# The second product of 43 token tiles by seven half-size products (Strassen), with the block sums of the squares on VectorE

## Chip, cores, metric

One core of one Trainium2 chip. The metric is the device time of one launch in microseconds (us); lower is better. Engines: TensorE (PE; PEld is its weight load), VectorE (DVE), ScalarE (ACT), GpSimd (POOL), and SyncE (SP), which here only issues DMAs.

## What is computed

The input is 8 sequences of 3008 positions with 256 channels. Each is Fourier transformed along its positions, mixed over the channels with complex weights, soft-thresholded and transformed back. The 8 x 3008 = 24064 results are tokens of a dense layer with a squared-ReLU:

```python
X = np.fft.rfft(x, axis=1)
Yr = Xr @ w_r - Xi @ w_i + b_r           # and Yi alike
Yr = np.sign(Yr) * np.maximum(np.abs(Yr) - 0.01, 0.0)
y = np.fft.irfft(Y, n=3008, axis=1).reshape(24064, 256)
r = np.maximum(y @ w_in, 0.0)            # w_in 256 x 2048: the first product
out = (s * (r * r) + b) @ w_out          # w_out 2048 x 256: the second product
```

The second product holds for g = r * r alone: s and the constant b times the column sums of w_out are brought in when the result leaves PSUM (s_bc, bias_bc).

## The kernel before

**Transforms.** 3008 = 94 x 32, so a transform is two stages of small matrix products with a transposition through DRAM between them. The work on batch b comes in units: s1_units (first forward stage, tile u, line 582), s23_units (second forward stage L618, channel mixing L633 and L647, soft threshold on VectorE L652 to L659 in the tile ring, first inverse stage L677) and s4_units (last inverse stage L730, tile yt). Most results leave PSUM through evac (L170 on ScalarE, L174 on VectorE). The first batch is transformed ahead of everything by first_batch, in the first 46 us. Units take their PSUM banks from one_bank (psf, two banks).

**Dense layer.** The tokens are cut into 48 tiles, mostly 512 tokens: 12 "wide" tiles (batches 0 and 1, of 512 or 480 tokens), 30 "main" tiles and 6 "tail" tiles (of 512 or 384), in the order of _tile_order. For tile ti, first_mm(ti, mc) computes one of MC = 16 blocks of 128 hidden features: two matmuls of 512 columns (L781) into half of a two-bank PSUM tile psh (two of those). After every second block ScalarE takes the ReLU of both into rt (f32, three buffers, L788), and the square goes to gt (f16), on VectorE (L795) or on ScalarE (L792). A tile's gt is eight buffers of 1024 columns; there are 15.

The second product of tile ti-1 runs while tile ti's first product does. Its stationary operand is gt, 128 features by up to 128 tokens, its moving operand a 256-column row block of w_out (L852). A sub-tile of 128 (or 120) tokens takes 16 matmuls that accumulate in half of a bank psa (two banks); two sub-tiles share a bank. VectorE then forms psa * s + bias into ost (L862), and SP stores it.

**Order.** The loop at the end writes the order by hand. Each tile has 16 slots, one for each mc: a slot issues the planned units of the transforms, then first_mm, then its share of the other tile's second product, four matmuls:

```python
for mc in range(MC):
    if ti < ti_n:
        for u in plan.pop(ti * MC + mc, []):
            u()
        first_mm(ti, mc)
    for u in nxt[mc * per_slot : (mc + 1) * per_slot]:
        u()
```

Where a job could go to either of ScalarE and VectorE, a planner decides when the program is built: load holds the time booked on both, and the job goes where its end is earlier by the planner's costs. For the squares:

```python
if load["act"] + 0.25 + w / 600.0 < load["dve"]:
    nc.scalar.activation(out=gt[:, :, 0:w], in_=rt[:, :, 0:w], func=AF.Square)
```

Each engine runs its instructions in order. When the program is built, the instructions of one engine may still change places with neighbours that they don't depend on.

Of the kernel before, what the change touches and what calls it, by code (L numbers as in the profile page):

```python
# [9 lines left out]
F16 = mybir.dt.float16  # L10
F32 = mybir.dt.float32
# [85 lines left out]
def kernel(  # L97
# [99 lines left out]
    def other_bank():  # L197
        return apool.tile([P, 512], F32, name="psa", tag="psa")
# [5 lines left out]
    def emit_load_x(b, first=None):  # L204
        xv = x[b].rearrange("(n1 n2) d -> n1 (n2 d)", n2=N2)
        for c in range(N2 // XCH):
            t = xpool.tile([P, XCH * D], F16, name="x16", tag="x16")
# [29 lines left out]
        nc.sync.dma_start(out=st, in_=w.rearrange("(c p) e -> p c e", p=P))  # L237
        w_st.append(st)

    b_g = cpool.tile([P, 2, D], F32, name="b_g")  # L240
# [6 lines left out]
    b_h = cpool.tile([P, D], F16, name="b_h")  # L247
# [4 lines left out]
    sel_t = cpool.tile([P, P], F16, name="sel_t")  # L252
    eye_t = cpool.tile([P, P], F16, name="eye_t")
    C_t = cpool.tile([96, 96], F16, name="C_t")

    b_st = rpool.tile([P, 2, D], F32, name="b_st", tag="rt")
# [79 lines left out]
            nc.vector.tensor_copy(out=blocks(F_2[0])[r, q, 1, a], in_=F_c[r, q, 0])  # L336


    w_sum = cpool.tile([P, 2, D], F16, name="w_sum")

    def sum_w_out():
        acc = opool.tile([P, 2, D], F32, name="acc", tag="ost")
# [6 lines left out]
    def make_bias():  # L349
        ps = other_bank()  # L350
        for i in range(2):
            nc.tensor.matmul(ps[:, 0:D], ones, w_sum[:, i], start=(i == 0), stop=(i == 1))
        nc.scalar.activation(out=bias_bc, in_=ps[:, 0:D], func=AF.Copy, scale=bb_bc)

    us = {}
    vs = {}
# [358 lines left out]
    def s4_units(b):  # L715

        groups = []
        for lo in range(0, N2, 5):
            for ec in range(DC):
                groups.append((lo, min(5, N2 - lo), ec))  # L720

        def unit(g):
            n2, w, ec = groups[g]
            if g == 0:
                yts[b] = ypool.tile([P, DC, N2, 96], F16, name="yt", tag="yt")
            yt = yts[b]
            ps = one_bank()
            for j in range(w):
                h, k = divmod(n2 + j, HW)
                nc.tensor.matmul(  # L730
                    ps[:, j * 96 : (j + 1) * 96],
                    vs[(b, h)][:, k, ec * P : (ec + 1) * P], C_t,
                    start=True, stop=True,
                )
            evac(
                yt[:, ec, n2 : n2 + w, :],
                ps[:, 0 : w * 96].rearrange("p (j n) -> p j n", n=96), w * 96,
            )
# [29 lines left out]
    def first_mm(ti, mc):  # L768
        tl = tiles[ti]
        w = width(tl)  # L770
        if mc % 2 == 0:
            hold_h["ps"] = two_banks()
        ps = hold_h["ps"]
        for dc in range(DC):
            o = ps[:, mc % 2, 0:w]
            r = rhs_of(tl, dc)
            if tl[0] == "main":
                o = o.rearrange("p (n m) -> p n m", m=16)
            if tl[0] == "wide":
# [8 lines left out]
        nc.scalar.activation(out=rt[:, :, 0:w], in_=ps[:, :, 0:w], func=AF.Relu)  # L788
        gt = gpool.tile([P, 2, 512], F16, name="gt", tag="gt")
        load["act"] += 0.17 + w / 600.0  # L790
        if load["act"] + 0.25 + w / 600.0 < load["dve"]:
            nc.scalar.activation(out=gt[:, :, 0:w], in_=rt[:, :, 0:w], func=AF.Square)  # L792
            load["act"] += 0.25 + w / 600.0
        else:
            nc.vector.tensor_tensor(  # L795
                out=gt[:, :, 0:w], in0=rt[:, :, 0:w], in1=rt[:, :, 0:w], op=ALU.mult
            )
            load["dve"] += 0.15 + w / 480.0
        gts[(ti, mc // 2)] = gt

    def store(tl, sub, src):
        kind, b, j, w = tl
        if kind == "wide":
# [33 lines left out]
    def second_mms(ti):  # L837

        tl = tiles[ti]
        w = width(tl)  # L840
        size = sub_size(tl)
        nsub = -(-w // size)
        hold = {}

        def mm(sub, mc):

            alone = ti == len(tiles) - 1 and sub >= 2
            h = 0 if alone else sub % 2
            if h == 0 and mc == 0:
                hold["ps"] = other_bank().rearrange("p (h e) -> p h e", h=2)  # L850
            ps = hold["ps"]
            nc.tensor.matmul(  # L852
                ps[0:size, h, :], gts[(ti, mc // 2)][:, mc % 2, sub * size : (sub + 1) * size],
                w_out_t[:, mc, :],
                start=(mc == 0), stop=(mc == MC - 1),
            )
            if sub == nsub - 1 and mc % 2 == 1:
                gts.pop((ti, mc // 2))
            if mc == MC - 1 and (alone or h == 1 or sub == nsub - 1):
                k = h + 1  # L860
                ost = opool.tile([P, 2, D], F32, name="ost", tag="ost")
                nc.vector.scalar_tensor_tensor(  # L862
                    out=ost[0:size, 0:k], in0=ps[0:size, 0:k], scalar=s_bc[0:size],
                    in1=bias_bc[0:size].unsqueeze(1).to_broadcast([size, k, D]), op0=ALU.mult, op1=ALU.add,
                )
# [4 lines left out]
        return [lambda s=s, m=m: mm(s, m) for s in range(nsub) for m in range(MC)]  # L870
# [24 lines left out]
    schedule(17, 10, rest[4:])  # L895
    plan.setdefault(14, []).append(make_bias)
    plan.setdefault(18, []).append(load_x_2)
    schedule(24, 42, s23_units(1))
    schedule(mark[1] - 12, 16, s4_units(1))
    for b in range(2, B):  # L900
# [8 lines left out]

    ti_n = len(tiles)  # L910
    for ti in range(ti_n + 1):
        nxt = second_mms(ti - 1) if ti else []
        per_slot = -(-len(nxt) // MC)
        for mc in range(MC):
            if ti < ti_n:
                for u in plan.pop(ti * MC + mc, []):
                    u()
                first_mm(ti, mc)
            for u in nxt[mc * per_slot : (mc + 1) * per_slot]:
                u()  # L920
    assert not plan

# [29 lines left out]
```

## Time and profile before

| | |
|---|---|
| three timed runs | 846.21, 847.24 (median), 849.21 us |
| span of the profiled execution | 844.6 us; the median run is 2.6 us longer, what lies around the span |
| PE busy | 835.1 us (99%), clock granted 1.00 but for the first 46 us (0.96) |
| VectorE, ScalarE busy | 694.7 us (82%), 640.6 us (76%) |
| main loop, 46 to 831 us | 785.2 us: PE 784.0, VectorE 654.5, ScalarE 604.0 |
| matmuls of the second product (L852) | 3024 |
| squares on VectorE, on ScalarE | 319, 65 |
| HBM traffic | 119 GB/s over the span |

Busy time is the union of an engine's instructions, so where two overlap they count once. A duration is from start to end; on TensorE, VectorE and ScalarE the next independent instruction starts before that end, and the distance between starts is what an instruction costs its engine.

### The profile page before, as it was taken

Reading aid. Unit: us, or ns where it says so; the run is one execution under the profiler, and the core shown is the slowest. Engines: PE = TensorE matmul, PEld = TensorE weight load, DVE = VectorE, ACT = ScalarE, POOL = GpSimd, SP = SyncE. Lnnn points to the kernel's source line nnn. Section 1 sums busy time; section 2 is a strip of 40 time slices with the busy share of each in tenths; the row PEclk is TensorE's granted clock in tenths of the full one; section 3 lists DMA queues with packets and bytes.
Section 4 is the critical chain, followed back from the end, with each engine's and each line's share of the span. In section 5 each row is a group of like instructions: output and inputs, shape, how many; then the busy total and the mean of one; then the engine's idle time right before and its main releaser. Section 6 shows DMA issues by size and latency. Waiting matters only on the chain.

```text
span 844.6 us, 17119 instructions
## 1 busy us (share of the span) xinstructions
PE 835.1 (99%) x6654; PEld 601.3 (71%) x6654; DVE 694.7 (82%) x1034; ACT 640.6 (76%) x862; POOL 45.9 (5%) x73
## 2 busy tenths in 40 slices
PE   8999999999999999999999999999999999999998
PEld 7857767777677766777677776777667777766765
DVE  5999987888888988888888888798978888776674
ACT  5987887778778877788777787778877778666673
POOL 4630000000000001000000000000000000000000
PEclk9999999999999999999999999999999999999999
DMA  7955467224851367324761247613354223411111
GB/s 200 181 151 118 119 161 199 74 77 98 202 156 54 103 171 188 93 70 107 189 174 50 81 101 196 172 43 90 106 152 125 59 78 97 113 33 38 38 44 50
DMA packets 105939, 96.06 MB, mean 114 GB/s; under 512 B 9607, under 2 KB 97675, under 8 KB 104515
## 3 DMA queue, kind: packets, MB, share of 16 engines
q1 hardware_dynamic: 99362, 80.55, 32.9%
q0 software_dynamic: 6496, 14.42, 10.6%
q8 instruction: 52, 0.85, 0.4%
q14 instruction: 29, 0.23, 0.1%
HBM read 53.52 MB, written 46.66 MB: 119 GB/s over the span
## 4 chain that ended last, share of the span: by engine, by line
PE 92%; ACT 3%; DVE 2%; DMA 1%; issue 1%; POOL 0%; DVEq 0%; ACTq 0%; POOLq 0%
PE psa L852 38%; PE psh L781 37%; PE psf L647 4%; PE psf L582 3%; PE psf L633 2%; PE psf L677 2%; PE psf L618 2%; PE psf L730 2%; ACT rt L788 1%; DMA x<-in_x_dram 1%; PE psm L425 1%; POOL x L213 0%; ACT yt L170 0%; DVE z L463 0%; PE psf L456 0%
## 5 line engine op out<-in xcount | busy, mean ns | idle before, releaser
L788 ACT ACTIVATE rt<-psh 128x1024 f32<-128x1024 f32 (+2 forms) x384 | 387.2, 1009 | 120.2 <-PE psh L781 118.8
L795 DVE TENSOR_TENSOR gt<-rt 128x1024 f16<-128x1024 f32 (+2 forms) x319 | 382.3, 1202 | 94.4 <-ACT rt L788 93.4
L852 PE MATMUL psa<-w_out_t,gt 128*128 128x256 f16 (+1 forms) x3024 | 454.4, 272 | 0.1
L852 PEld LDWEIGHTS <-gt 128*128 128x128 f16 (+1 forms) x3024 | 300.9, 101 | 186.6 <-issue 1.1
L781 PE MATMUL psh<-yt,w_in 128*128 128x512 f16 (+1 forms) x1344 | 396.8, 378 | 0.2 <-ACT rt L788 0.2
L781 PEld LDWEIGHTS <-w_in 128*128 128x128 f16 x1536 | 142.7, 98 | 26.2 <-issue 1.2
L862 DVE SCALAR_TENSOR_TENSOR ost<-psa,s_bc,bias_bc 128x512 f32<-128x512 f32 (+2 forms) x97 | 71.1, 733 | 9.6 <-PE psa L852 7.9
L792 ACT ACTIVATE gt<-rt 128x1024 f16<-128x1024 f32 (+2 forms) x65 | 68.2, 1050 | 0.9
L652 DVE TENSOR_TENSOR ring<-psf,s 128x512 f16<-128x512 f32 x84 | 57.6, 685 | 3.3 <-PE psf L647 3.2
L170 ACT CAST v<-psf 128x512 f16<-128x512 f32 x77 | 44.8, 582 | 19.4 <-PE psf L677 19.4
L170 ACT CAST xf<-psf 128x512 f16<-128x512 f32 x79 | 46.3, 586 | 8.8 <-PE psf L618 8.8
L781 PE MATMUL psh<-tail,w_in 128*128 128x512 f16 (+1 forms) x192 | 52.1, 353 | 0.0
L170 ACT CAST u<-psf 96x512 f16<-96x512 f32 x74 | 42.8, 580 | 11.2 <-PE psf L582 10.9
L647 PE MATMUL psf<-W_g,xf 128*128 128x256 f16 x336 | 50.4, 273 | 0.0
L170 ACT CAST yt<-psf 128x480 f16<-128x480 f32 (+2 forms) x76 | 39.0, 520 | 14.7 <-PE psf L730 14.2
L213 POOL DMA_DIRECT2D x<-in_x_dram x36 | 18.8, 527 | 432.9 <-PE psf L582 431.7
L582 PE MATMUL psf<-x,A_t 94*96 94x512 f16 x102 | 38.9, 382 | 1.0 <-ACT yt L170 0.6
L658 DVE TENSOR_TENSOR ring<-ring,high 128x512 f16<-128x512 f16 x84 | 35.6, 423 | 2.3
L659 DVE TENSOR_TENSOR ring<-ring 128x512 f16<-128x512 f16 x84 | 35.6, 423 | 2.1
L657 DVE TENSOR_TENSOR ring<-ring,low 128x512 f16<-128x512 f16 x84 | 35.5, 422 | 1.6
L647 PEld LDWEIGHTS <-xf 128*128 128x128 f16 x336 | 32.9, 98 | 4.1 <-issue 0.2
L730 PE MATMUL psf<-C_t,vs 96*128 96x96 f16 x448 | 33.2, 205 | 0.0
(100 smaller groups left out, 508.6 us busy)
## 6 DMA issues: line engine op xcount, KB each, us to landing
out_dram<-ost SPq DMA_DIRECT2D x152, 128.0 KB
ud<-u SPq DMA_DIRECT2D x28, 384.0 KB
us<-ud SPq DMA_DIRECT2D x28, 384.0 KB
vd<-v SPq DMA_DIRECT2D x42, 256.0 KB
vs<-vd SPq DMA_DIRECT2D x14, 768.0 KB
x<-in_x_dram POOLq DMA_DIRECT2D x28, 376.0 KB, 6.3
ring<-ring SPq DMA_DIRECT2D x280, 32.0 KB
out_dram<-ost SPq DMA_DIRECT2D x16, 120.0 KB
```

The costliest lines, as they stand in the source:

```text
L170: return None, nc.scalar.copy(out=dst, in_=src)
L582: nc.tensor.matmul(ps[0:96, :], A_t[0:N1, :], x16[(b, c)][0:N1, j * D : (j + 2) * D], start=True, stop=True,)
L647: nc.tensor.matmul(ps[:, r, :], xt[:, 2 - r, dc], W_g[:, dc, r], start=(dc == 0), stop=(dc == DC - 1),)
L652: nc.vector.tensor_tensor(out=t, in0=ps, in1=hold[i // 2][:, i % 2].unsqueeze(1).to_broadcast([P, 2, D]), op=ALU.add,)
L658: nc.vector.tensor_tensor(out=m, in0=m, in1=high, op=ALU.min)
L730: nc.tensor.matmul(ps[:, j * 96 : (j + 1) * 96], vs[(b, h)][:, k, ec * P : (ec + 1) * P], C_t, start=True, stop=True,)
L781: nc.tensor.matmul(o, w_in_t[dc][:, mc * P : (mc + 1) * P], r, start=(dc == 0), stop=(dc == DC - 1),)
L788: nc.scalar.activation(out=rt[:, :, 0:w], in_=ps[:, :, 0:w], func=AF.Relu)
L792: nc.scalar.activation(out=gt[:, :, 0:w], in_=rt[:, :, 0:w], func=AF.Square)
L795: nc.vector.tensor_tensor(out=gt[:, :, 0:w], in0=rt[:, :, 0:w], in1=rt[:, :, 0:w], op=ALU.mult)
L852: nc.tensor.matmul(ps[0:size, h, :], gts[(ti, mc // 2)][:, mc % 2, sub * size : (sub + 1) * size], w_out_t[:, mc, :], start=(mc == 0), sto ...
L862: nc.vector.scalar_tensor_tensor(out=ost[0:size, 0:k], in0=ps[0:size, 0:k], scalar=s_bc[0:size], in1=bias_bc[0:size].unsqueeze(1).to_broad ...
```

## The change

For 43 tiles (all of 512 or 480 tokens but the first and the last tile) the second product is seen as a 2 x 2 block product. The tile's tokens are halved (i), its 16 feature blocks are split into even and odd ones (k: the two that share a square), and the 256 output columns are halved. With A(i,k) the squares and B(k,j) the weights, Strassen's method in Winograd's form needs seven products of half size in every direction instead of eight:

- s_op makes four block sums of the squares in f16 on VectorE, each in two halves q of the features: S1 = A21 + A22 into new buffers s1, S3 = A11 - A21, S2 = S1 - A11 and S4 = A12 - S2 in place of blocks of gt.
- make_t makes the four block differences T of w_out once, on GpSimd.
- seven_mms issues 7 products x 2 sub-tiles x 8 feature blocks = 112 matmuls of 128 columns, seven per slot, into four bank fills per tile (psa still has two banks); leave(bank) then adds up the products with seven scaled adds from PSUM (add) and two adds in SBUF (both) per tile.
- The first tile, the last one, and the tail tiles of 384 tokens keep second_mms.
- gt becomes buffers of half a tile (four). To make room, the pools of x, u, xf and v lose one buffer each, and some constants share buffers. yt is computed with 94 columns per position rather than 96.

The planner books the new VectorE work, 0.07 + size / 480 for a block sum, 0.4 for add, 0.35 for both. The core of the diff:

```diff
-    xpool = ctx.enter_context(tc.tile_pool(name="xp", bufs=4))
-    upool = ctx.enter_context(tc.tile_pool(name="up", bufs=3))
+    xpool = ctx.enter_context(tc.tile_pool(name="xp", bufs=3))
+    x2pool = ctx.enter_context(tc.tile_pool(name="xp2", bufs=1))
+    upool = ctx.enter_context(tc.tile_pool(name="up", bufs=2))
-    xfpool = ctx.enter_context(tc.tile_pool(name="xfp", bufs=4))
+    xfpool = ctx.enter_context(tc.tile_pool(name="xfp", bufs=3))
-    vpool = ctx.enter_context(tc.tile_pool(name="vp", bufs=3))
+    vpool = ctx.enter_context(tc.tile_pool(name="vp", bufs=2))
-    gpool = ctx.enter_context(tc.tile_pool(name="gp", bufs=15))
-    opool = ctx.enter_context(tc.tile_pool(name="op", bufs=3))
+    gpool = ctx.enter_context(tc.tile_pool(name="gp", bufs=4))
+    opool = ctx.enter_context(tc.tile_pool(name="op", bufs=4))
+    spool = ctx.enter_context(tc.tile_pool(name="sp", bufs=2))
+    zpool = ctx.enter_context(tc.tile_pool(name="zp", bufs=1))
...
+    def w_block(k, j):
+        return w_out_t.rearrange("p (q k) d -> p q k d", k=2)[:, :, k, j * P : (j + 1) * P]
+
+    def make_t(i):
+        if not T_s:
+            T_s.append(x2pool.tile([P, 4, MC // 2, P], F16, name="T_s", tag="x2"))
+        t = T_s[0]
+        a, b = (
+            (w_block(0, 1), w_block(0, 0)),
+            (w_block(1, 1), t[:, 0]),
+            (w_block(1, 1), w_block(0, 1)),
+            (w_block(1, 0), t[:, 1]),
+        )[i]
+        nc.gpsimd.tensor_tensor(out=t[:, i], in0=a, in1=b, op=ALU.subtract)
...
-        gt = gpool.tile([P, 2, 512], F16, name="gt", tag="gt")
+        q, g = divmod(mc // 2, 4)
+        if g == 0:
+            gts[(ti, q)] = gpool.tile([P, 4, 2, 512], F16, name="gt", tag="gt")
+        gt = gts[(ti, q)][:, g]
...
+    def part(ti, q, i, k):
+        size = 2 * sub_size(tiles[ti])
+        return gts[(ti, q)][:, :, k, i * size : (i + 1) * size]
+
+    def s_op(ti, n, q):
+        size = 2 * sub_size(tiles[ti])
+        if n == 1:
+            sums[(ti, q)] = spool.tile([P, 4, 2 * P], F16, name="s1", tag="s1")
+        s1 = sums[(ti, q)][:, :, 0:size]
+        a11, a12, a21, a22 = (part(ti, q, i, k) for i in range(2) for k in range(2))
+        out, a, b, op = {
+            1: (s1, a21, a22, ALU.add),
+            3: (a21, a11, a21, ALU.subtract),
+            2: (a11, s1, a11, ALU.subtract),
+            4: (a12, a12, a11, ALU.subtract),
+        }[n]
+        nc.vector.tensor_tensor(out=out, in0=a, in1=b, op=op)
+        load["dve"] += 0.07 + size / 480.0
+
+    def seven_mms(ti):
+        left = [("g", 0, 0), ("g", 0, 1), ("s", 0, 0), ("g", 0, 0), ("g", 1, 0), ("g", 1, 1), ("g", 0, 1)]
+        right = [w_block(0, 0), w_block(1, 0)] + [T_s[0][:, i] for i in (0, 1, 2, 3)] + [w_block(1, 1)]
+
+        def mm(n, j, c):
+            if n % 2 == 0 and j == 0 and c == 0:
+                hold[n // 2] = other_bank().rearrange("p (n j e) -> p n j e", n=2, j=2)
...
+            nc.tensor.matmul(
+                hold[n // 2][0:size, n % 2, j], lhs, right[n][:, c],
+                start=(n % 2 == 0 and j == 0 and c == 0), stop=(c == MC // 2 - 1),
+                skip_group_check=True,
+            )
+
+        def add(out, n, other):
+            nc.vector.scalar_tensor_tensor(
+                out=out, in0=hold[n // 2][0:size, n % 2], scalar=s_bc[0:size],
+                in1=other, op0=ALU.mult, op1=ALU.add,
+            )
+            load["dve"] += 0.4
+
+        def both(out, a, b):
+            nc.vector.tensor_tensor(out=out, in0=a, in1=b, op=ALU.add)
+            load["dve"] += 0.35
...
+            if bank == 0:
+                add(c22, 0, wide(bias_bc))
+                add(c11, 1, c22)
+            elif bank == 1:
+                add(c22, 3, c22)
+                add(z, 2, wide(b_21))
+                both(c12, c22, z)
+            elif bank == 2:
+                add(c22, 4, c22)
+                add(c21, 5, c22)
+                both(c22, c22, z)
+                for j in range(2):
+                    store(tl, 2 + j, hold["o", 1][:, j, :])
+            else:
+                add(c12, 6, c12)
+                for j in range(2):
+                    store(tl, j, hold["o", 0][:, j, :])
+
+        C = MC // 2
+        order = [(n, j, c) for n in range(2) for j in range(2) for c in range(C - 1)]
+        order += [(n, j, C - 1) for n in range(2) for j in range(2)]
+        order += [(n, j, c) for n in range(2, 7) for j in range(2) for c in range(C)]
+        slots = [[] for _ in range(MC)]
+        for at, what in enumerate(order):
+            slots[at // 7].append(lambda w=what: mm(*w))
+        for at, n, q in ((3, 1, 1), (4, 3, 1), (4, 2, 0), (5, 2, 1), (7, 4, 0), (8, 4, 1)):
+            slots[at].append(lambda n=n, q=q: s_op(ti, n, q))
+        for at, bank in ((6, 0), (9, 1), (13, 2), (15, 3)):
+            slots[at].append(lambda bank=bank: leave(bank))
+        return slots
...
+        if ti:
+            nxt = seven_mms(ti - 1) if seven(ti - 1) else second_mms(ti - 1)
...
                 first_mm(ti, mc)
+                if mc in (9, 10) and seven(ti):
+                    s_op(ti, 1 if mc == 9 else 3, 0)
```

In the changed kernel's line numbers, s_op's instruction is L922, the 128-column matmul L944, add L951, both L958, the square on VectorE L826, the first product L809.

More of the change, by code (lines that the diff above doesn't have):

```diff
@@ L206, in emit_load_x @@
         for c in range(N2 // XCH):
-            t = xpool.tile([P, XCH * D], F16, name="x16", tag="x16")
+            if b < 2 and c == N2 // XCH - 1:
+                t = x2pool.tile([P, XCH * D], F16, name="x2", tag="x2")
+            else:
+                t = xpool.tile([P, XCH * D], F16, name="x16", tag="x16")
             if first is not None:
@@ L238 @@
         w_st.append(st)
-    b_g = cpool.tile([P, 2, D], F32, name="b_g")
+    b_g = tpool.tile([P, 2, D], F32, name="b_g", tag="tail")
+    small = tpool.tile([P, 4, D], F16, name="small", tag="tail")
     nc.vector.memset(b_g, 0.0)
@@ L246 @@
     F_2 = [uspool.tile([P, H, P], F16, name="F_2", tag="us") for _ in range(2)]
-    b_h = cpool.tile([P, D], F16, name="b_h")
+    b_h = small[:, 0]
     nc.vector.memset(b_h, 0.0)
@@ L251 @@
         nc.gpsimd.dma_start(out=b_h[64 * i : 64 * i + 1], in_=bv.unsqueeze(0))
-    sel_t = cpool.tile([P, P], F16, name="sel_t")
-    eye_t = cpool.tile([P, P], F16, name="eye_t")
+    sel_t = small[:, 1, 0:P]
+    eye_t = small[:, 1, P:D]
     C_t = cpool.tile([96, 96], F16, name="C_t")
@@ L336, in place_f @@
             nc.vector.tensor_copy(out=blocks(F_2[0])[r, q, 1, a], in_=F_c[r, q, 0])
-    w_sum = cpool.tile([P, 2, D], F16, name="w_sum")
+    w_sum = small[:, 2:4]
+    b_21 = cpool.tile([P, P], F32, name="b_21")
+    T_s = []
+    def w_block(k, j):
[11 more added lines that the diff above has]
+        nc.gpsimd.tensor_tensor(out=t[:, i], in0=a, in1=b, op=ALU.subtract)
     def sum_w_out():
@@ L353, in make_bias @@
         nc.scalar.activation(out=bias_bc, in_=ps[:, 0:D], func=AF.Copy, scale=bb_bc)
+        nc.gpsimd.tensor_tensor(
+            out=b_21, in0=bias_bc[:, P:D], in1=bias_bc[:, 0:P], op=ALU.subtract
+        )
     us = {}
@@ L730, in unit @@
                 nc.tensor.matmul(
-                    ps[:, j * 96 : (j + 1) * 96],
-                    vs[(b, h)][:, k, ec * P : (ec + 1) * P], C_t,
+                    ps[:, j * N1 : (j + 1) * N1],
+                    vs[(b, h)][:, k, ec * P : (ec + 1) * P], C_t[:, 0:N1],
                     start=True, stop=True,
@@ L735, in unit @@
             evac(
-                yt[:, ec, n2 : n2 + w, :],
-                ps[:, 0 : w * 96].rearrange("p (j n) -> p j n", n=96), w * 96,
+                yt[:, ec, n2 : n2 + w, 0:N1],
+                ps[:, 0 : w * N1].rearrange("p (j n) -> p j n", n=N1), w * N1,
             )
@@ L798, in first_mm @@
             load["dve"] += 0.15 + w / 480.0
-        gts[(ti, mc // 2)] = gt
     def store(tl, sub, src):
@@ L839, in second_mms @@
         tl = tiles[ti]
-        w = width(tl)
         size = sub_size(tl)
-        nsub = -(-w // size)
+        nsub = -(-tl[3] * (16 if tl[0] == "wide" else 1) // size)
         hold = {}
@@ L852, in mm @@
             nc.tensor.matmul(
-                ps[0:size, h, :], gts[(ti, mc // 2)][:, mc % 2, sub * size : (sub + 1) * size],
+                ps[0:size, h, :],
+                gts[(ti, mc // 8)][:, mc // 2 % 4, mc % 2, sub * size : (sub + 1) * size],
                 w_out_t[:, mc, :],
@@ L856, in mm @@
             )
-            if sub == nsub - 1 and mc % 2 == 1:
-                gts.pop((ti, mc // 2))
             if mc == MC - 1 and (alone or h == 1 or sub == nsub - 1):
@@ L868, in mm @@
                     store(tl, sub - k + 1 + i, ost[:, i, :])
-        return [lambda s=s, m=m: mm(s, m) for s in range(nsub) for m in range(MC)]
+        units = [lambda s=s, m=m: mm(s, m) for s in range(nsub) for m in range(MC)]
+        per_slot = -(-len(units) // MC)
+        return [units[i * per_slot : (i + 1) * per_slot] for i in range(MC)]
+    sums = {}
+    def part(ti, q, i, k):
[15 more added lines that the diff above has]
+        load["dve"] += 0.07 + size / 480.0
@@ new lines, in seven_mms, with wide, leave @@
+    def seven_mms(ti):
+        tl = tiles[ti]
+        size = sub_size(tl)
+        hold = {}
+        left = [("g", 0, 0), ("g", 0, 1), ("s", 0, 0), ("g", 0, 0), ("g", 1, 0), ("g", 1, 1), ("g", 0, 1)]
[3 more added lines that the diff above has]
+                hold[n // 2] = other_bank().rearrange("p (n j e) -> p n j e", n=2, j=2)
+            kind, i, k = left[n]
+            q, g = divmod(c, 4)
+            if kind == "s":
+                lhs = sums[(ti, q)][:, g, j * size : (j + 1) * size]
+            else:
+                at = (2 * i + j) * size
+                lhs = gts[(ti, q)][:, g, k, at : at + size]
+            nc.tensor.matmul(
[7 more added lines that the diff above has]
+                in1=other, op0=ALU.mult, op1=ALU.add,
+            )
+            load["dve"] += 0.4
+        def both(out, a, b):
+            nc.vector.tensor_tensor(out=out, in0=a, in1=b, op=ALU.add)
+            load["dve"] += 0.35
+        def wide(t):
+            return t[0:size, 0:P].unsqueeze(1).to_broadcast([size, 2, P])
+        def leave(bank):
+            if bank == 0:
+                for i in range(2):
+                    hold["o", i] = opool.tile([P, 2, D], F32, name="ost", tag="ost")
+                hold["z"] = zpool.tile([P, 2, P], F32, name="zz", tag="zz")
+            (c11, c12), (c21, c22) = (
+                (hold["o", i][0:size, :, 0:P], hold["o", i][0:size, :, P:D]) for i in range(2)
+            )
+            z = hold["z"][0:size]
+            if bank == 0:
+                add(c22, 0, wide(bias_bc))
[10 more added lines that the diff above has]
+                    store(tl, 2 + j, hold["o", 1][:, j, :])
+            else:
+                add(c12, 6, c12)
[13 more added lines that the diff above has]
+        return slots
@@ L873, with seven @@
+    def seven(ti):
+        tl = tiles[ti]
+        return 1 <= ti < len(tiles) - 1 and (tl[0] == "wide" or tl[3] == 512)
     plan = {}
@@ L897 @@
     plan.setdefault(18, []).append(load_x_2)
+    for i in range(4):
+        plan.setdefault(15 + i, []).append(lambda i=i: make_t(i))
     schedule(24, 42, s23_units(1))
@@ L911 @@
     for ti in range(ti_n + 1):
-        nxt = second_mms(ti - 1) if ti else []
-        per_slot = -(-len(nxt) // MC)
+        nxt = [[]] * MC
+        if ti:
+            nxt = seven_mms(ti - 1) if seven(ti - 1) else second_mms(ti - 1)
         for mc in range(MC):
@@ L918 @@
                 first_mm(ti, mc)
-            for u in nxt[mc * per_slot : (mc + 1) * per_slot]:
+                if mc in (9, 10) and seven(ti):
+                    s_op(ti, 1 if mc == 9 else 3, 0)
+            for u in nxt[mc]:
                 u()
```

## The prediction

> **What bounds the kernel now.** I read the engine totals first, then the chain, then the costliest groups, then the same totals over the stretch that the change touches.
>
> ```profile
> span 844.6 us, 17119 instructions
> PE 835.1 (99%) x6654; PEld 601.3 (71%) x6654; DVE 694.7 (82%) x1034; ACT 640.6 (76%) x862; POOL 45.9 (5%) x73
> ...
> PE 92%; ACT 3%; DVE 2%; DMA 1%; issue 1%; POOL 0%; DVEq 0%; ACTq 0%; POOLq 0%
> ```
>
> TensorE is busy for 99% of the span and is 92% of the chain, so it is the bound. VectorE has only 18% to spare: about 150 us. The windows show how that is spread: the main loop (46 to 831 us), and its stretch where VectorE is busiest.
>
> ```profile
> core 0: us, PE busy (x) PEld busy (x) DVE busy (x) ACT busy (x) POOL busy (x), PEclk, DMA share, GB/s
> 46.00:831.20 785.20, 784.01 (x6069) 558.09 (x6068) 654.51 (x954) 603.95 (x796) 19.74 (x35) 1.00 0.42 110
> 98.30:115.80 17.50, 17.45 (x124) 12.74 (x123) 16.68 (x33) 15.08 (x22) 0.52 (x1) 1.00 0.62 153
> ```
>
> In the loop PE has 784.0 of 785.2 us, VectorE 654.5, ScalarE 604.0. The fullest stretch has VectorE at 16.68 of 17.50 us, 95.3%, with PE still running: that is the fullest that this kernel shows VectorE.
>
> **TensorE, what is removed.** One tile's second product is 64 matmuls of 256 columns; it becomes 7 x 2 x 8 = 112 matmuls of 128 columns, each with its own weight load. What one costs is not its duration (they are pipelined) but the distance between starts.
>
> ```profile
> 300.25 0.60 PE L852 MATMUL psa<-w_out_t,gt 128*128 128x256 f16 x4
> 300.69 0.38 PE L582 MATMUL psf<-x,A_t 94*96 94x512 f16 x1
> ```
>
> ```profile
> 23.31 0.22 PE L456 MATMUL psf<-g,F_t 128*128 128x128 f16 x1
> 23.37 0.22 PE L456 MATMUL psf<-g,F 128*128 128x128 f16 x1
> 23.43 0.22 PE L456 MATMUL psf<-g,F_t 128*128 128x128 f16 x1
> 23.48 0.22 PE L456 MATMUL psf<-g,F 128*128 128x128 f16 x1
> ```
>
> Four 256-wide ones take 300.25 to 300.69; the trace's median distance is 0.109 us. The 128-wide ones of L456, which load new weights (F_t, F) every time, start 0.055 to 0.06 us apart; I take 0.0555. Per tile 64 x 0.109 = 6.98 against 112 x 0.0555 = 6.22: 0.76 us less, and 43 tiles give 32.7 us. The inverse transform's columns (96 to 94) are worth under 1 us. PE's need in the loop falls from 784 to 751 us.
>
> The Trainium skill speaks against this step: its page "TensorE: Matmul & The Clock Gate", section "Back-to-back issue gap", gives about 81 ns per matmul for a sustained stream of weight load and matmul at 128 columns. By that the tile would be 9.07 us, and PE would gain 90 us of work in the loop. The rows above show 55 ns in this kernel, so I go by them.
>
> **VectorE, what is removed and added.** Counts are from the built order of both kernels, durations from these rows (columns: count, then busy us and mean ns of one):
>
> ```profile
> L795 DVE TENSOR_TENSOR gt<-rt 128x1024 f16<-128x1024 f32 x271 | 330.1, 1222 | 81.8 <-ACT rt L788 81.1
> L862 DVE SCALAR_TENSOR_TENSOR ost<-psa,s_bc,bias_bc 128x512 f32<-128x512 f32 x84 | 62.7, 747 | 7.5 <-PE psa L852 5.9
> L658 DVE TENSOR_TENSOR ring<-ring,high 128x512 f16<-128x512 f16 x84 | 35.6, 423 | 2.3
> L624 DVE TENSOR_TENSOR xf<-xf 128x256 f16<-128x256 f16 x84 | 23.6, 286 | 6.4 <-ACT xf L170 6.1
> L862 DVE SCALAR_TENSOR_TENSOR ost<-psa,s_bc,bias_bc 128x256 f32<-128x256 f32 x5 | 2.4, 480 | 1.8 <-PE psa L852 1.8
> ```
>
> ```profile
> 22.07 0.68 DVE L434 TENSOR_TENSOR g<-psm,b_g 128x512 f16<-128x512 f32 x1
> 22.66 0.68 DVE L174 CAST vt<-psa 128x512 f16<-128x512 f32 x1
> 23.26 0.68 DVE L463 SCALAR_TENSOR_TENSOR z<-psf,m 128x512 f16<-128x512 f32 x1
> ```
>
> The last three lines show that independent instructions overlap: 0.68 us long, 0.60 apart. In the trace the median overlap is 0.084 us, so every price below is the mean less 0.084.
>
> Removed. The planner (load) moves squares to ScalarE, since it books the new VectorE work: L795 falls from 319 to 212, 95 of 1024 elements at 1.138, 8 of 960 at 1.087 and 4 of 768 at 0.898, 120.4 us. Evacuations move too: 19 of u and 7 of v at 0.598, 20 of yt at 0.57, 27.0 us. 86 evacuations L862 go, at 0.663: 57.0 us. Together 204.4.
>
> Added. (1) Block sums, s_op: eight per tile, 312 of 4x256 and 32 of 4x240 f16. No row has this width. The f16 rows give 286 ns at 256 and 423 at 512, so 137 per 256 more: 697 at 1024, 0.613 us after the overlap (0.579 at 960): 209.8 us. Bounds: 0.339 (the 512 row, as if more width cost nothing) and 1.138 (the f32 square of the same width), 117 to 391 us; I take the line through the two f16 rows, the nearest in type. (2) Seven scaled adds from PSUM per tile, 301 of 256 elements: the 256-wide L862 row gives 0.396 us, 119.2 us. (3) Two f32 adds in SBUF per tile, 86: between 0.202 (L624) and 0.396; the middle, 0.30, 25.8 us. Together 354.8.
>
> (4) Order. An instruction that reads what the one just ahead of it wrote waits instead of overlapping. The built order has 191 such places before and 77 after, since the new work is placed between the ring operations: 114 x 0.084 = 9.6 us back.
>
> VectorE's need in the loop: 654.5 - 204.4 + 354.8 - 9.6 = 795 us, against 751 for PE and a loop that now takes 785. So VectorE becomes the bound. ScalarE gets 107 squares (0.96 each after its own 0.105 overlap, from L792's 1064 ns) and 46 evacuations (about 0.47): 604 + 103 + 22 = 729 us, below both.
>
> **The sum.** VectorE cannot be full all the time; I give it the fullest stretch's share, 95.3%: 795.3 / 0.953 = 834.5 us for the loop, 49.3 more than now. Span 844.6 + 49.3 = 893.9. The three timed runs have a median of 847.24, 2.6 above the profiled span; kept, it makes 896.5, so 896 us. Per tile that is 1.1 us more, where PE alone would have saved 0.76.
>
> **Edits at nothing.** The smaller pools (x, u, xf, v): each buffer's last reader stands at least one unit ahead of the next writer in PE's order; without that cover one evacuation, 0.6 us, would wait per unit. gt in halves, four buffers: the first square of a tile reuses the half that PE left in the previous slot. make_t: four POOL operations, by L344's 1155 ns for half their width about 9 us, in slots 15 to 18, used some 15 slots later; behind them in POOL's queue stand batch 2's x loads, needed over 20 slots later. Stores: still four per tile on SP, now at slots 13 and 15 rather than 7 and 15; the ring and v transfers queued behind them wait for the last adds, 1 to 2 us, and have several units of slack.
>
> **New waits.** Two PSUM banks serve four bank fills per tile. The next tile's first matmul needs the third bank's three adds, which VectorE can start only when PE is 16 matmuls from the tile's end (some 2 us). Behind them in VectorE's queue is the last add, which waits for the tile's last matmul. So VectorE may lag PE by about two slots at the tile's end, and squares, sums and evacuations all stand behind. In the first slots of a tile it has little to do until PE and ScalarE deliver.
>
> **Rivals.**
> Coupling costs more than the 95.3% allows (0.22): the wait just described leaves VectorE idle for another 1 us per tile, 43 us: 940. For it: both directions are tight within a tile. Against: in 98 to 116 us VectorE was at 95% without PE stopping.
> PE stays the bound (0.08, the faster side): the place is s_op. If a 4x256 sum cost at most about 0.465 us, VectorE's need would be 744, at 95.3% under the present loop; at 0.375 it is 713, PE decides, and the time is 844.6 - 32.7 + 2.6 = 814. A VectorE without any idle time at my prices would give 844.6 + 10 + 2.6 = 857, still slower. Against: two f16 rows on one line.
> Weight loads bind (0.04): if a load's 98 ns could not be hidden behind 128 columns, the tile would take 11.0 us and the loop 785 + 173: 1020. Against: L456.
> No measurable change (0.02): between those.
> The forecast, VectorE at 92 to 100%: 857 to 925, chance 0.64.
>
> Within 0.3% (2.5 us) this kernel's runs, which spread over 3 us, cannot tell a change. Faster 0.08, same 0.02, slower 0.90. The range for 8 in 10 is 852 to 942: it leaves out most of the faster side and the weight-load case.
>
> **What would show it.** Right: VectorE at 93 to 97% of the loop, PE at 88 to 91%, new waits of L944 matmuls or their loads for VectorE, the chain mostly VectorE; L922 near 700 ns; 128-wide L944 at 55 ns. Wrong: L922 under 550 ns, or PE still at 99%; or L944 at 80 ns or more, PE full and the time over 900.

## The result, and the profile after

The changed kernel takes **878.38 us** (median of four runs, 877.69 to 881.0), the kernel before 846.99 us beside it: ratio 1.0372, 95% interval 1.0352 to 1.0392. The forecast of 896 us had the sign and the engine right and was 18 us too high. The profiled execution took 878.36 us with a span of 876.6.

First the span, the engine totals and the chain from the page of the changed kernel:

```profile
span 876.6 us, 21884 instructions
PE 823.5 (94%) x8718; PEld 600.8 (69%) x8718; DVE 825.9 (94%) x1527; ACT 755.9 (86%) x1014; POOL 60.6 (7%) x78
...
DVE 46%; PE 26%; DMA 10%; ACT 8%; issue 7%; SPq 1%; POOL 0%; DVEq 0%; ACTq 0%; POOLq 0%
```

TensorE made up 92% of the chain and now makes up 26%; VectorE went from 2% to 46%. Next its windows: the main loop, the first 17.5 us of that, one full stretch, and the end of the loop, where the transforms are done.

```profile
core 0: us, PE busy (x) PEld busy (x) DVE busy (x) ACT busy (x) POOL busy (x), PEclk, DMA share, GB/s
46.00:863.00 817.00, 773.01 (x8123) 558.64 (x8122) 786.29 (x1446) 718.40 (x947) 35.85 (x41) 0.99 0.41 106
46.00:63.50 17.50, 12.00 (x61) 6.12 (x60) 16.25 (x11) 10.09 (x14) 13.56 (x8) 0.81 0.48 135
360.10:377.60 17.50, 17.04 (x188) 12.81 (x187) 17.47 (x39) 15.88 (x20) 0.00 (x0) 1.00 0.19 56
758.00:855.00 97.00, 94.24 (x973) 66.59 (x971) 85.10 (x128) 81.05 (x94) 1.07 (x1) 1.00 0.13 38
```

VectorE is busy for 786.3 of 817.0 us of the loop, 96.2%, and for 17.47 of 17.50 us in the full stretch. Before, the fullest stretch shown had 95.3%. The second row is the one that no step of the prediction foresaw: at the start of the loop TensorE has only 12.0 of 17.5 us, at a granted clock of 0.81, with GpSimd busy for 13.6. In the last row VectorE has 88%; from the same matmul of the first product to the same one, these last tiles take 97.0 us for 96.0 before.

The costliest groups by form (count, then busy us and mean ns of one, then idle time ahead of them):

```profile
L826 DVE TENSOR_TENSOR gt<-rt 128x1024 f16<-128x1024 f32 x176 | 220.9, 1258 | 18.4 <-ACT rt L816 17.9
L944 PE MATMUL psa<-w_out_t,gt 128*128 128x128 f16 x1872 | 158.9, 220 | 6.3 <-DVE zz L951 4.6 <-DVE gt L826 1.3
L944 PE MATMUL psa<-T_s,gt 128*128 128x128 f16 x1872 | 157.3, 219 | 9.5 <-DVE gt L922 8.7 <-DVE ost L951 0.6
L922 DVE TENSOR_TENSOR gt<-gt 128x1024 f16<-128x1024 f16 x156 | 105.6, 681 | 0.3
L951 DVE SCALAR_TENSOR_TENSOR ost<-psa,s_bc,ost 128x256 f32<-128x256 f32 x195 | 92.5, 477 | 4.9 <-PE psa L944 2.9
L958 DVE TENSOR_TENSOR ost<-ost,zz 128x256 f32<-128x256 f32 x78 | 32.6, 417 | 0.3
```

A block sum (L922) takes 681 ns, and VectorE idled only 0.3 us ahead of all 156 of this form. The matmuls L944 now wait for VectorE: for block sums, and for the adds that free a PSUM bank (L951).

**TensorE's time, taken apart.** Each distance between the starts of two matmuls is split into what a matmul of that width takes back to back (nominal) and the excess. Excess of 60 ns or more goes to the engine whose instruction ended just before; excess at half clock stands by itself; short gaps make the remainder, and in e9 some 14 us of waits for transfers too. From 46 us to 13 us before the end, in us:

| kernel | loop | nominal | waits for VectorE | waits for ScalarE | at half clock |
|---|---|---|---|---|---|
| before | 785.5 | 776.7 | 1.0 | 3.7 | 0 |
| changed | 817.5 | 743.9 | 46.6 | 16.3 | 4.3 |
| sums left out (e2) | 780.3 | 745.9 | 7.9 | 17.4 | 1.6 |
| sums left out, unbooked (e12) | 785.1 | 744.7 | 13.7 | 13.8 | 4.6 |
| f16 ReLU output (e6) | 789.2 | 744.1 | 21.7 | 11.8 | 4.5 |
| more VectorE work (e9) | 861.6 | 744.1 | 31.7 | 57.8 | 9.3 |
| all four edits (e7) | 778.2 | 744.3 | 12.9 | 14.4 | 0 |

TensorE's own time fell by 32.8 us, and its waits for VectorE rose by 45.6, for ScalarE by 12.6, with 4.3 at half clock. Together they make 29.7 of the 32 us by which the loop is longer; the other 2.3 lie in short gaps.

### The profile page after: what moved, and what is told of

Its sections match the earlier page's. It is cut to its first block, busy times and chain, and to the rows that moved or that the text cites. A ratio compares the mean times of both kernels' runs of the same rounds, so it can differ in the third digit from the quotient of the medians.

```text
span 876.6 us, 21884 instructions
## 1 busy us (share of the span) xinstructions
PE 823.5 (94%) x8718; PEld 600.8 (69%) x8718; DVE 825.9 (94%) x1527; ACT 755.9 (86%) x1014; POOL 60.6 (7%) x78
## 4 chain that ended last, share of the span: by engine, by line
DVE 46%; PE 26%; DMA 10%; ACT 8%; issue 7%; SPq 1%; POOL 0%; DVEq 0%; ACTq 0%; POOLq 0%
DVE gt L826 12%; PE psh L809 9%; DVE gt L922 8%; PE psa L944 8%; DVE ost L951 5%; DVE ring L680 4%; ACT rt L816 4%; DVE s L922 3%; DMA out_dram<-ost 3%; DMA ring<-ring 3%; DVE ring L685 2%; DVE ring L686 2%; DVE ring L687 2%; PE psf L758 2%; PE psa L880 2%
## 5 line engine op out<-in xcount | busy, mean ns | idle before, releaser
L816 ACT ACTIVATE rt<-psh 128x1024 f32<-128x1024 f32 (+2 forms) x384 | 386.8, 1009 | 64.4 <-PE psh L809 59.3
L809 PE MATMUL psh<-yt,w_in 128*128 128x512 f16 (+1 forms) x1344 | 401.2, 380 | 0.9 <-ACT rt L816 0.9
L944 PEld LDWEIGHTS <-gt 128*128 128x128 f16 (+1 forms) x4128 | 287.8, 101 | 160.0 <-DVE gt L922 15.1
L826 DVE TENSOR_TENSOR gt<-rt 128x1024 f16<-128x1024 f32 (+2 forms) x212 | 259.6, 1227 | 20.4 <-ACT rt L816 19.8
L823 ACT ACTIVATE gt<-rt 128x1024 f16<-128x1024 f32 (+2 forms) x172 | 181.0, 1052 | 2.4
L944 PE MATMUL psa<-w_out_t,gt 128*128 128x128 f16 (+1 forms) x2064 | 175.3, 219 | 8.0 <-DVE zz L951 6.3
L944 PE MATMUL psa<-T_s,gt 128*128 128x128 f16 (+1 forms) x2064 | 173.4, 219 | 9.5 <-DVE gt L922 8.7
L809 PEld LDWEIGHTS <-w_in 128*128 128x128 f16 x1536 | 132.4, 98 | 27.1 <-issue 7.8
L922 DVE TENSOR_TENSOR gt<-gt 128x1024 f16<-128x1024 f16 (+1 forms) x172 | 115.9, 678 | 0.3
L951 DVE SCALAR_TENSOR_TENSOR ost<-psa,s_bc,ost 128x256 f32<-128x256 f32 (+1 forms) x215 | 102.0, 477 | 5.0 <-PE psa L944 2.9
L944 PEld LDWEIGHTS <-s 128*128 128x128 f16 (+1 forms) x688 | 48.0, 101 | 20.4 <-DVE s L922 1.6
L944 PE MATMUL psa<-T_s,s 128*128 128x128 f16 (+1 forms) x688 | 59.8, 219 | 0.7 <-DVE s L922 0.7
L922 DVE TENSOR_TENSOR s<-gt 128x1024 f16<-128x1024 f16 (+1 forms) x86 | 58.5, 680 | 1.1 <-ACT gt L823 0.6
L922 DVE TENSOR_TENSOR gt<-s,gt 128x1024 f16<-128x1024 f16 (+1 forms) x86 | 58.3, 679 | 0.0
L809 PE MATMUL psh<-tail,w_in 128*128 128x512 f16 (+1 forms) x192 | 52.4, 353 | 0.0
L173 ACT CAST yt<-psf 128x470 f16<-128x470 f32 (+2 forms) x95 | 48.4, 528 | 4.6 <-PE psf L758 2.9
```

The source lines that it names most:

```text
L173: return None, nc.scalar.copy(out=dst, in_=src)
L809: nc.tensor.matmul(o, w_in_t[dc][:, mc * P : (mc + 1) * P], r, start=(dc == 0), stop=(dc == DC - 1),)
L826: nc.vector.tensor_tensor(out=gt[:, :, 0:w], in0=rt[:, :, 0:w], in1=rt[:, :, 0:w], op=ALU.mult)
L922: nc.vector.tensor_tensor(out=out, in0=a, in1=b, op=op)
L944: nc.tensor.matmul(hold[n // 2][0:size, n % 2, j], lhs, right[n][:, c], start=(n % 2 == 0 and j == 0 and c == 0), stop=(c == MC // 2 - 1), ...
L951: nc.vector.scalar_tensor_tensor(out=out, in0=hold[n // 2][0:size, n % 2], scalar=s_bc[0:size], in1=other, op0=ALU.mult, op1=ALU.add,)
```

## The experiments

Theory A: VectorE's block sums and adds hold the loop, so the time follows VectorE's need. Against it stood single collisions at places where the prediction put edits at nothing, hand-offs and bank waits that cost time at any load of VectorE, and ScalarE as the next bound. The first experiment looks for a collision, the others raise or lower VectorE's need in several ways.

**e1: the block differences of w_out on VectorE, not on GpSimd.**

```diff
-        nc.gpsimd.tensor_tensor(out=t[:, i], in0=a, in1=b, op=ALU.subtract)
+        nc.vector.tensor_tensor(out=t[:, i], in0=a, in1=b, op=ALU.subtract)
```

> The changed kernel, with the four differences of the weights (make_t) made on VectorE instead of GpSimd. Theory A: the first tile's loss of 8.6 us comes from GpSimd and VectorE working in each other's way in the same memory while make_t runs; on VectorE the four take about 0.6 us each, so the first tile's step falls from 8.6 to 0 to 3 us and the time from 878 to 869 to 873 us. Rival B: the first tile is slow for another reason (shared buffers, constants that come late); the time stays within 2 us of 878.

Why it was tried: the timelines of the changed kernel, VectorE's and then GpSimd's (start, us, engine, line, operation, count).

```profile
47.95 9.27 DVE L826 TENSOR_TENSOR gt<-rt 128x1024 f16<-128x1024 f32 x3 [0.49 <-ACT rt L816]
57.15 0.68 DVE L177 CAST vs<-psf 96x512 f16<-96x512 f32 x1
```

```profile
47.89 5.19 POOL L364 TENSOR_TENSOR T_s<-w_out_t 128x1024 f16<-128x1024 f16 x2 [0.47 <-PE psa L610]
53.04 6.17 POOL L364 TENSOR_TENSOR T_s<-w_out_t,T_s 128x1024 f16<-128x1024 f16 x2
```

And the kernel before at the same place, VectorE's timeline:

```profile
47.81 4.67 DVE L795 TENSOR_TENSOR gt<-rt 128x1024 f16<-128x1024 f32 x4 [1.43 <-ACT rt L788]
```

Before, four squares took 4.67 us. Beside the four GpSimd operations three take 9.27 us, 3.1 each. The evacuation that TensorE needs (L177, 57.15) stands behind them; TensorE waits 4.6 us for it and then runs at half clock until 63.8.

The Trainium skill has this in "GPSIMD Engine Reference", section 1 "Specifications": GpSimd and VectorE share their SBUF interfaces, and VectorE instructions with two SBUF inputs are among those that collide there. The page gives no size; the two timelines above agree with it.

Measured: 877.03 us (874.51 to 879.7), ratio 1.0356 (1.0331 to 1.0381). The squares there take 1.15 us again, but the time missed the expectation: the medians are 1.4 us apart, less than the runs of either kernel spread. Followed matmul by matmul of the first product (L809), e1 enters the loop 2.5 us later than the changed kernel (its granted clock was 0.5 from 14.9 to 18.3 us, the other's 1.00). At 76 us it is 4.7 us ahead, so the place of the collision took 7.2 us less. At 123 us 0.2 of the 4.7 are left. A window of this run shows where they went:

```profile
118.00:126.00 8.00, 6.20 (x45) 3.96 (x46) 3.95 (x11) 3.71 (x6) 0.00 (x0) 0.79 0.59 172
```

TensorE had waited over 3 us for a transfer into the ring tile (L705), and ran at a clock of 0.79 here, which the changed kernel does not do at this place. From 150 us on the two runs go in parallel, 0.6 to 0.8 us apart. So the collision is real and costs 7 us where it happens. That most of this is lost again fits a loop held by VectorE's total, which is only 5 us smaller here, but no run shows that it is the reason.

**e2: the block sums left out** (on e1; the planner still books them).

```diff
-            sums[(ti, q)] = spool.tile([P, 4, 2 * P], F16, name="s1", tag="s1")
...
-        nc.vector.tensor_tensor(out=out, in0=a, in1=b, op=op)
...
-        left = [("g", 0, 0), ("g", 0, 1), ("s", 0, 0), ("g", 0, 0), ("g", 1, 0), ("g", 1, 1), ("g", 0, 1)]
+        left = [("g", 0, 0), ("g", 0, 1), ("g", 1, 0), ("g", 0, 0), ("g", 1, 0), ("g", 1, 1), ("g", 0, 1)]
```

> As the run with make_t on VectorE, and the block sums of the squares are left out: the products read unsummed blocks, so the output is another one; the planner still books them, so every other instruction keeps its engine. VectorE's need falls by 344 x 0.6 = 206 us to about 605 us of the loop. Theory A (VectorE's occupancy is the whole cost, the 128-column matmuls start every 55 ns): TensorE is the bound again, 844.6 - 32.7 + 2.6 = 814 us, up to 822 with some waits left; L944 has a median start distance of 55 to 56 ns. Rival C (hand-offs of the banks at the tile's end, or matmuls slower than 55 ns, cost the time): it stays above 840 us.

Measured: 838.45 us (837.6 to 841.38), ratio 0.9906 (0.9886 to 0.9926): 38.6 us less than e1, for 344 instructions. It lies between the two expectations, 16 us above A's and 1.5 below C's. The loop of this run:

```profile
46.00:825.00 779.00, 765.33 (x8133) 558.56 (x8131) 613.36 (x1110) 713.84 (x951) 24.95 (x37) 1.00 0.43 112
```

A is confirmed for the sign: without the sums the change gains. It is not the whole cost: 24 us of the gain expected are missing, and TensorE still waits 17.4 us for ScalarE and 7.9 for VectorE.

**e12: the same without the booking**, so that the planner gives squares back to VectorE.

```diff
-        load["dve"] += 0.07 + size / 480.0
```

> As the run without the block sums (they are left out, so the output is another one), but the planner does not book them either, so that squares and evacuations go back from ScalarE to VectorE. The run without sums stayed at 838 us, 24 above what TensorE alone allows, with ScalarE at 92% of the loop. If ScalarE's fullness is what held it, TensorE's waits for ScalarE (17 us there) fall under 8 and the time to 822 to 831; if the waits come from the order of the work or the small pools, it stays at 835 to 840.

Measured: 841.33 us (838.85 to 846.16), ratio 0.9909 (0.9885 to 0.9934), above both ranges expected. The loop:

```profile
46.00:828.00 782.00, 761.90 (x8097) 557.26 (x8097) 693.15 (x1202) 636.76 (x847) 25.28 (x37) 0.99 0.43 111
```

ScalarE fell from 713.8 to 636.8 us, and nothing was gained, so its fullness is not what held e2. What is left above TensorE's own time is hand-offs (matmuls that wait for one evacuation, one square or the add that frees their bank) and single stalls: 2.9 us at 234, where TensorE waited for the transfer vs<-vd, and 4.6 us at 329, where an evacuation to u waited for the transfer that empties its buffer. How these 24 us divide stays open.

**e9: more of the disputed work.** The first block sum of each half is made twice.

```diff
-        nc.vector.tensor_tensor(out=out, in0=a, in1=b, op=op)
+        for _ in range(2 if n == 1 else 1):
+            nc.vector.tensor_tensor(out=out, in0=a, in1=b, op=op)
```

> The changed kernel with the first block sum of every half made twice (86 more operations of 0.6 us on VectorE, 52 us, not booked by the planner); the result is the same. Theory A (VectorE sets the pace from end to end, fullness 96%): the time rises by 45 to 54 us, to 923 to 932. Rival C or a mixed bound (VectorE decides in part of the tiles only, ScalarE and hand-offs in the others): it rises by 15 to 35 us.

Measured: 922.16 us (921.62 to 926.02), ratio 1.0894 (1.0875 to 1.0913), 43.8 us over the changed kernel. The loop:

```profile
46.00:907.00 861.00, 800.94 (x8123) 557.80 (x8122) 831.57 (x1532) 717.10 (x947) 41.99 (x41) 0.99 0.38 101
```

86 instructions at 0.6 us are 52 us, of which 84% arrived; VectorE's busy time grew by 45.3 us and the loop by about as much. VectorE is idle for 29 us of this loop and for 31 of the changed kernel's: its idle time did not grow with its work. The table puts most of this run's waits down to ScalarE. In part these are VectorE's too: TensorE waits 26 us for a ReLU (L816), and the ReLUs themselves wait 10.2 us, in 11 places, for a square on VectorE to free an rt buffer.

The rise is 1 us under theory A's range and well over rival C's. But 11 of the 43.8 us arise in one stretch that VectorE does not hold:

```profile
347.20:396.90 49.70, 38.96 (x393) 26.98 (x392) 38.12 (x64) 29.94 (x42) 2.31 (x2) 0.90 0.38 103
```

The changed kernel goes from the same matmul to the same one in 38.7 us, with VectorE busy for 35.4. Here VectorE has 77%, ScalarE stands for 6.0 us for a transfer that empties u, and TensorE for 4.0 us for the transfer us<-ud. Outside this stretch VectorE's idle time falls from 27 us in the changed kernel to 18.

**e4 and e5: the planner's costs set to the measured distances** (e4 on e1; e5 on the kernel before, as a control).

```diff
-        ta, td = 0.17 + cols / 1200.0, 0.15 + cols / 960.0
+        ta, td = 0.04 + cols / 1200.0, 0.065 + cols / 960.0
...
-            load["act"] += 0.6
+            load["act"] += 0.47
...
-        load["act"] += 0.17 + w / 600.0
-        if load["act"] + 0.25 + w / 600.0 < load["dve"]:
+        load["act"] += 0.055 + w / 600.0
+        if load["act"] + 0.105 + w / 600.0 < load["dve"]:
...
-            load["act"] += 0.25 + w / 600.0
+            load["act"] += 0.105 + w / 600.0
...
-            load["dve"] += 0.15 + w / 480.0
+            load["dve"] += 0.065 + w / 480.0
```

> As the run with make_t on VectorE, and the planner's costs set to the distances between starts that the trace shows (evacuation 0.04 + cols/1200 and 0.065 + cols/960, ReLU 0.055, square 0.105 on ScalarE and 0.065 on VectorE, each plus the width term as before). Squares on VectorE fall from 212 to 168. VectorE's need in the loop falls by some 40 us to about 745 us, TensorE's is 751, ScalarE's about 765. Theory A (VectorE's occupancy sets the pace, about 96% can be filled): the loop falls to 785 to 800 us and the time to 842 to 858. Rival C (hand-offs): no more than 5 us under the run with make_t on VectorE alone. Rival D: ScalarE, now the fullest, becomes the bound, and the time is 855 to 870.

> The kernel before with the same new planner costs, as a control: 20 squares and some evacuations move to ScalarE. All theories: TensorE is the bound there, so 845 to 849 us, no change.

Measured: e4 870.09 us (868.37 to 871.14), ratio 1.0275 (1.0255 to 1.0294); e5 847.49 us, ratio 1.0003 (0.9993 to 1.0013). e4's totals and chain:

```profile
PE 824.6 (95%) x8718; PEld 602.6 (69%) x8718; DVE 777.8 (90%) x1473; ACT 794.5 (92%) x1072; POOL 57.1 (7%) x74
...
ACT 31%; PE 30%; DVE 25%; issue 8%; DMA 4%; POOL 0%; SPq 0%; DVEq 0%; ACTq 0%; POOLq 0%
```

Seven us came back over e1, well short of theory A's 842 to 858 and at the upper end of rival D's 855 to 870. VectorE at 90% and ScalarE at 92% hold TensorE in turns: work handed from one to the other does not help much when both are nearly full. The control shows no difference.

**e6 and e8: the ReLU's output rt in f16 rather than f32** (e6 on the changed kernel; e8 on the kernel before, as a control).

```diff
-        rt = rpool.tile([P, 2, 512], F32, name="rt", tag="rt")
+        rt = rpool.tile([P, 2, 512], F16, name="rt", tag="rt")
...
-            load["dve"] += 0.15 + w / 480.0
+            load["dve"] += 0.07 + w / 960.0
```

> The changed kernel with one thing more: the ReLU result rt is f16 instead of f32, so a square on VectorE is an f16 operation of 1024 elements (0.60 us from start to start, as the block sums) rather than 1.13, and the planner books 0.07 + w/960 for it. Nothing of the seven products is touched. VectorE's need falls by about 48 us (268 squares, but at half the price, and more evacuations), ScalarE's by about 42. Theory A (the seven products save TensorE 33 us, and the loss is the occupancy of VectorE and ScalarE): the waits of TensorE for both fall from 63 to some 25 us and the time to 830 to 848. Rival C (the hand-off of banks and sums at the tile's ends is the cost, whatever the engines' load): above 865.

> The kernel before with rt in f16 and the planner's cost for it, as a control: VectorE and ScalarE get lighter by 60 and 100 us, TensorE stays the bound. All theories: 844 to 848 us, no change beyond 0.3%.

Measured: e6 851.87 us (847.92 to 857.32), ratio 1.0051 (1.0027 to 1.0075), 26.5 us less than the changed kernel and 4 us above theory A's range; e8 848.58 us, ratio 1.0022 (1.0011 to 1.0034). The squares of e6 by form:

```profile
L826 DVE TENSOR_TENSOR gt<-rt 128x1024 f16<-128x1024 f16 x224 | 159.4, 713 | 22.8 <-ACT rt L816 21.6
```

713 ns for 1258. VectorE makes 56 more of the squares in all (268 for 212) and is still 49 us less busy in the loop. In the kernel before, where VectorE is not the bound, the same edit gains nothing. This is theory A from the other side: make VectorE's work cheaper without touching the seven products, and the loss is nearly gone. A cheaper square also comes sooner to the sums and matmuls behind it, and no run adds work to VectorE that nothing waits for. So that the cause is a full VectorE, and not a longer path through it, rests on the 96.2% of the changed kernel and not on these runs.

**e7, e10, e11: all four edits, and two of them taken back.** e7 has f16 rt, the block differences on VectorE, the planner's measured costs and a third u buffer:

```diff
-    upool = ctx.enter_context(tc.tile_pool(name="up", bufs=2))
+    upool = ctx.enter_context(tc.tile_pool(name="up", bufs=3))
```

e10 is e7 with two u buffers; e11 is e7 with the block differences on GpSimd.

> As the run with rt in f16, and make_t on VectorE, the planner's costs set to the trace's distances between starts, and a third buffer for u (there is room for it once rt is f16). Theory A: VectorE and ScalarE both have about 700 us of need in the loop against 744 for TensorE, the stall at 337 us for the transfer of u goes, and so does the first tile's; 822 to 838 us, faster than before. Rival C: above 860.

> The run with all four edits (839 us), but with two buffers for u again, as in the changed kernel. The question is what the lost buffer costs by itself. If the stall of TensorE near 337 us (an evacuation to u waits for a transfer out of u) comes from the missing buffer, it returns: 2.4 us of wait and 3.4 us at half clock, so 842 to 845 us. If it came from VectorE running late, as everything else does, it stays away and the time is 838 to 841.

> The run with all four edits, but with make_t on GpSimd again. If GpSimd and VectorE hold each other up while make_t runs, the squares of the first tile take longer than the 0.68 us of the other tiles, and 2 to 9 us are lost in the first tile, so 841 to 848 us; with f16 squares the loss may be smaller than the 8.6 us of the changed kernel. If make_t on GpSimd is harmless: 838 to 841.

| kernel | median us (lowest to highest) | ratio to the kernel before (95%) |
|---|---|---|
| e7 | 839.29 (839.01 to 840.3) | 0.9909 (0.9895 to 0.9924) |
| e10 | 846.13 (844.54 to 849.38) | 0.9987 (0.9968 to 1.0006) |
| e11 | 847.03 (846.15 to 848.8) | 0.9992 (0.9982 to 1.0002) |

e7 beats both kernels, though it stays 1.3 us above the range expected; e10 is 1.1 us above the range for a missing buffer, and e11 is within its own. e7's totals and chain, then its loop:

```profile
span 837.3 us, 21906 instructions
PE 813.3 (97%) x8718; PEld 600.0 (72%) x8718; DVE 734.1 (88%) x1538; ACT 747.2 (89%) x1007; POOL 46.3 (6%) x74
...
PE 54%; ACT 23%; DVE 13%; issue 5%; DMA 4%; POOL 0%; DVEq 0%; SPq 0%; ACTq 0%; POOLq 0%
```

```profile
46.00:824.00 778.00, 763.81 (x8131) 558.28 (x8130) 695.04 (x1457) 710.50 (x940) 22.04 (x37) 1.00 0.42 111
```

TensorE leads the chain again, and the loop is 7 us shorter than before, with VectorE at 89% of it and ScalarE at 91%.

In e7 VectorE no longer holds the loop, and the two collisions can be priced there. In e11 the GpSimd operations cost 7.7 us of median. VectorE's timeline of e11:

```profile
48.30 4.85 DVE L826 TENSOR_TENSOR gt<-rt 128x1024 f16<-128x1024 f16 x2
53.07 0.68 DVE L177 CAST u<-psa 96x512 f16<-96x512 f32 x1
53.67 4.53 DVE L826 TENSOR_TENSOR gt<-rt 128x1024 f16<-128x1024 f16 x2
58.12 0.68 DVE L177 CAST vs<-psf 96x512 f16<-96x512 f32 x1
58.72 0.67 DVE L826 TENSOR_TENSOR gt<-rt 128x1024 f16<-128x1024 f16 x1
```

Four f16 squares take 2.3 to 2.4 us each, the fifth, which comes after GpSimd has ended, 0.67. The evacuation between them, with one input from PSUM, keeps its 0.68. By the first stores of the loop, at 77 us, e11 is 6.6 us behind e7, and it stays there.

In e10 the missing u buffer costs 6.8 us. TensorE's timeline of e10, and ScalarE's of the changed kernel at its own such place:

```profile
324.44 0.37 PE L758 MATMUL psf<-C_t,vs 96*128 96x94 f16 x5
327.73 0.37 PE L758 MATMUL psf<-C_t,vs 96*128 96x94 f16 x5 [2.92 <-ACT u L173]
```

```profile
334.47 1.05 ACT L816 ACTIVATE rt<-psh 128x1024 f32<-128x1024 f32 x1
338.66 0.58 ACT L173 CAST u<-psf 96x512 f16<-96x512 f32 x1 [3.13 <-DMA ud<-u]
```

An evacuation to u has to wait for the transfer that empties the buffer (8.4 us long in the chain of the changed kernel), ScalarE stands for 3.1 us, and TensorE, which needs the bank that the evacuation frees, for 2.9 in e10. Followed matmul by matmul, e10 loses 3.0 us to e7 here. Another 2.5 us are lost by 57 us, and there ScalarE waits for the same transfer:

```profile
46.15 0.58 ACT L173 CAST u<-psm 96x512 f16<-96x512 f32 x1 [1.26 <-DMA ud<-u]
```

VectorE waits 1.4 us for it beside ScalarE, TensorE enters the loop 1.5 us later than in e7, and the granted clock was 0.5 from 46.8 to 50.2 us. e7 has neither the wait nor the half clock, so the buffer is the likely cause of these 2.5 us too; it is read from one profile of each.

## Why the prediction was right, and where its sizes were off

- **TensorE's saving: right.** 32.7 us predicted; 32.8 by the table's nominal times, 30.5 if the short gaps are counted with them. The 128-column matmuls start 55 to 56 ns apart, against the 55.5 taken from L456, so the rows of L456 were the right witness. The rival "weight loads bind" is out. The Trainium skill's 81 ns ("TensorE: Matmul & The Clock Gate", "Back-to-back issue gap") did not hold in these 4368 matmuls; the measurement decides.
- **VectorE's new work: right.** A block sum: 681 ns predicted at 697, and 0.602 us from start to start for 0.613. A scaled add: 0.395 for 0.396. An f32 add in SBUF: 0.336 for 0.30, so the middle was 3 us too low over 86.
- **VectorE's need: 795 predicted, 786 measured**, and of the latter some 7 us are the squares that GpSimd slowed. The rest of the gap, 16 us, must lie in the terms for removed work and for order. One reason that the records allow: I took the 0.084 us of overlap off every removed instruction, while before only 489 of VectorE's 954 instructions in the loop began before the previous one's end. Those without overlap were worth more than I took off. No run singled this out.
- **VectorE as the bound: right.** It is 96.2% full in the loop; I had said 93 to 97%. Its share of the chain is 46%, the largest, where I had said mostly. TensorE's busy time in the loop is 94.6% (I had said 88 to 91%). The smaller loss explains only part of that, 751 of 817.5 being 92%. The rest is the measure: a recorded duration (219 ns for 128 columns, 56 from start to start) reaches some 160 ns into each wait. By the nominal times TensorE works for 91% of the loop.
- **The step that was mis-sized: "VectorE cannot be full all the time; I give it 95.3%".** The loop is 817, not 834.5. Half of the 17 us is the need above. The other half is the fullness: 17.47 of 17.50 us in a stretch is possible, and VectorE was idle for 31 us of the loop where the division allowed 39. The fullest stretch of a kernel in which VectorE is not the bound was no ceiling: in e9, with still more work, it is idle for 29 us, and outside one stretch for 18 rather than 27.
- **Coupling: out.** The wait for a PSUM bank exists (L944 behind L951, 10 us in 17 waits, up to 1.9 us), but not the 43 us more that the rival asked for.
- **"PE stays the bound": out for this change.** Its point was a block sum of 0.465 us or less; it costs 0.602. The price of 814 us for that case was too low as well: with no sums at all the kernel takes 838, since hand-offs keep TensorE waiting.
- **Edits at nothing: two of them were wrong, and the forecast was lucky.** make_t on GpSimd was costed by GpSimd's own queue alone, and I did not ask what it does to VectorE's squares beside it. The smaller pools were said to have a unit's cover; the u buffer's transfer takes longer than that cover near 330 us. Followed matmul by matmul of the first product, the changed kernel is 7.8 us behind the kernel before at 81 us, past the first place, and loses 4.3 us more from 335 to 344 us, at the second: 12 of the 32 us, at two terms that the sum puts at nothing. If these 12 us are taken as their cost, the sum was 30 us too high for the work that it does price, and the two errors partly cancelled. What taking these places away is worth differs: 1.4 us of median for the first in the changed kernel (e1), 7.7 and 6.8 in e7. No run gives the changed kernel its u buffer back alone.
- **One bound was mis-added.** 795.3 us at 92% makes 926.5 us in all, not 925; nothing hangs on it.

## What to carry to other kernels

Before moving work off a full engine, set what is saved there (0.76 us per tile here) against the start-to-start cost of what is added to the next fullest, and let that engine be fuller than it has been seen: 95.3% was the most before, 96.2% is the whole loop after. If it comes out over, make that engine's work cheaper first: with f16 ReLU output, planner costs as measured, no GpSimd work beside two-input VectorE work and one buffer given back, the same seven products go from 3.7% slower to 0.9% faster. Buffers taken away and operations sent to an idle engine show up as single stalls: look for them in the timeline, since their price in the median changes with what else holds the loop (1.4 us for the GpSimd operations in the changed kernel, 7.7 in e7).

## What the runs showed of the hardware

- GpSimd element-wise work on 1024 f16 columns (2.3 to 3.1 us each) slows a VectorE square beside it from 1.15 to 3.1 us (f32 input) and from 0.67 us to between 2.3 and 2.6 (f16 input, e11 and e6), but not a cast from PSUM (0.68 us).
- A TensorE stall can cost more than itself: with waits of 4.6 us (to 57.9) and 2.2 us (to 339.3) in the changed kernel the granted clock was 0.5 from 57.0 to 63.8 and from 340.3 to 343.7 us. Not every stall does that: after one of 2.9 us in e10 (to 327.7) the granted clock stayed 1.00. What decides stays open.
- Matmuls of 128 columns, each with new weights, run at 55 to 56 ns from start to start for a whole loop; a recorded duration of 219 ns says nothing of that.
